# Cross network on one core: product 3 by seven small products in one more layer of pair A, layer 4 of pair B summed by DMA, the next input's transposes held back

## The chip, the cores and the metric

The kernel runs on one core of a Trainium2 chip. Five engines work side by side and wait for each other by semaphores: TensorE (PE in the profile, matmuls into PSUM), VectorE (DVE), ScalarE (ACT), GpSimd (POOL) and SyncE (SP). Here ScalarE copies every matmul result from PSUM to SBUF, VectorE does the sums and multiplications on SBUF, SyncE issues all ordinary DMAs and the transposing ones, and GpSimd issues the DMAs that add to what lies in SBUF. Each engine works through its own instructions in program order. The metric is the device time of one execution in microseconds.

## The reference

```
B, F, D, L = 16384, 100, 16, 6          # Din = 1024, all bf16
x = x0
for l in range(L):
    proj = x @ ws[l] + bs[l]            # 16384x1024 by 1024x1024
    x = x0 * proj + x
```

## The kernel before, in words

**Tiling.** The 16384 rows are cut into 16 pairs of 1024 rows; a pair has two halves n = 0, 1 of 512 rows. States are kept transposed (features on partitions), so a pair's input x0T and its state xst are each a tile `big` of 128 x 2 x 8 x 512. Eight rounds s = 0 to 7 each take two pairs, A and B, through the six layers, alternating: A0, B0, A1, B1 and so on to A5, B5. One such step (pair, layer) is the unit of this text. Six `big` tiles hold the inputs and states of A and B and the next inputs; the next round's inputs go to the tiles nA and nB.

**Products.** A step's 1024x1024 by 1024x1024 product is made in seven half-size products (1 to 7) instead of eight, from sums of weight blocks and sums T13, T2, T4 of the state. From round 1 on, some of the seven are themselves made from seven products of 256x256 blocks: product 2 (`in2`), product 4 (`in4`) and product 3 (`in3`, `X.l, in3 = l, s > 0 and l < L - 1`, so in layers 0 to 4). A product by four matmul groups is `mm` (line 450, 512 columns); by seven small ones it is `inner` (line 458, 256 columns). Each needs block sums of the state by VectorE (`ti2`, `ti4`, `ti3`), combinations of the weights (ids 8, 9 and 10 for products 2, 4 and 3), and sums of partial results (`EA` and `EB`; `E4` and `e5`; `E3` and `e6`).

**Weights.** In round 0 the combinations are made by VectorE (`combo`) and written to the DRAM tensor `Lc` by a DMA on SyncE; combination 10 of layer l is made in step B l. From round 1 on, nine 512 KB weight tiles per layer come through a ring of nine buffers (`prefetch_upto`), loaded in B steps as the buffers of the layer come free, and combination 10 comes by `load_third` into the tile P2s (line 365), which has a single buffer.

**The end of a step.** A step leaves its result in P1s, U2s, S53, P5s and C2; the state's new value is x0 times a projection, plus the old state. This is finished partly in the step itself (`fin_of`: m0, a0) and partly in the next step of the other pair (`trail`: m1, s11, a1, mC2, aC2). For the layers that `by_dma` names, `return 0 < Y.l < L - 1 - Y.pr % 2`, three of the four sums are not VectorE's but DMAs that add to xst, issued by GpSimd (`dadd`, line 50): one from T2 in the step itself, then one from U2s (m1d) and one from C2 (m2d, shown as `cb`) in the next step. Y.pr is odd for pair B, so A has it in layers 1 to 4, B in layers 1 to 3.

**Inputs and outputs.** `bring` loads the next pair's input by two transposing DMAs (`load_x0`, line 224). It is called from the list `pending`, which a step runs right after it has asked for its first weights, so before nearly all of its other work: in A5 `bring("A")`, and in rounds 1 to 6 `bring("B")` too. In round 0 the input of B is brought at the start of the next step A0. A finished pair is turned back by a transposing DMA from xst to x0T (`turn_pair`, line 351, called by `end_of(Y, True)` in the next step, after `w6 = weights(6)`), and written out by two DMAs (`write_pair`, line 358) at the start of the step after that. All of these stand in SyncE's one queue, in the order in which the program calls them.

Of the kernel before, what the change touches and what calls it, by code (L numbers as in the profile page):

```python
# [17 lines left out]
def kernel(  # L18
# [7 lines left out]
    nc = tc.nc  # L26
    P = nc.NUM_PARTITIONS
    B, D = x0.shape
    L = ws.shape[0]
# [6 lines left out]
    NPAIR = B // PR  # L36
# [6 lines left out]
    pin = tc.keep_in_program_order  # L43

    def vtt(out, in0, in1, op):
        return pin(nc.vector.tensor_tensor(out=out, in0=in0, in1=in1, op=op))  # L46
# [27 lines left out]
    def bigt(i):  # L74
        return big.tile([P, 2, KD, NB], BF16, name=f"big{i}")
# [4 lines left out]
    def bank(p):  # L80
        return p.tile([P, NB], FP32, name="px")
# [17 lines left out]
    def prefetch_upto(n):  # L99
        while state["next"] < min(n, len(keys)):  # L100
            k = keys[state["next"]]
            W[k] = wtile()
            pin(nc.sync.dma_start(W[k][:], raw_src(k[1], k[2]) if k[2] in RAW else lc(k[1], k[2])))
            state["next"] += 1
# [6 lines left out]
    def alloc(l):  # L111
        for pid in (1, 2, 4):
            W[0, l, pid] = wtile()
        for i, pid in enumerate((6, 3, 7)):
            W[0, l, pid] = wtile() if l % 2 == 0 else quarter(extra, i)
        W[0, l, 8] = quarter(extra, 3)

    def load_raw(l, eng, pids):
        for pid in pids:
            if pid == 12:  # L120
                t = raw12[l] = ei_pool.tile([P, KH, H], BF16, name="ea")
            else:
                t = W[0, l, pid]
            pin(eng.dma_start(t[:], raw_src(l, pid)))

    def combo(l, pid):
        if pid <= 7:
            a, op, b = {5: (lambda: raw12[l], ADD, lambda: W[0, l, 4]), 6: (lambda: W[0, l, 5], SUB, lambda: W[0, l, 1]),
                        3: (lambda: W[0, l, 2], SUB, lambda: W[0, l, 6]), 7: (lambda: W[0, l, 1], SUB, lambda: raw12[l])}[pid]
            if pid == 5:  # L130
                W[0, l, 5] = ei_pool.tile([P, KH, H], BF16, name=("eb", "e4")[l % 2])
            t = W[0, l, pid]
            vtt(t[:], a()[:], b()[:], op)
        else:
            w = W[0, l, {8: 2, 9: 4, 10: 3}[pid]]
            t = W[0, l, 8] if pid == 8 else ti_pool.tile([P, KH, H], BF16, name="ti4")
            i11, i12, i21, i22 = w[:, 0:2, 0:HE], w[:, 0:2, HE:H], w[:, 2:4, 0:HE], w[:, 2:4, HE:H]
            iv = t[:].rearrange("p k (j e) -> p k j e", e=HE)
            vtt(iv[:, 0], i12, i22, ADD)
            vtt(iv[:, 3], i11, i12, SUB)  # L140
            vtt(iv[:, 1], iv[:, 0], i11, SUB)
            vtt(iv[:, 2], i21, iv[:, 1], SUB)
        pin(nc.sync.dma_start(lc(l, pid), t[:]))
# [65 lines left out]
    home = dict(xA=0, xB=1, sA=2, sB=3, nA=4, nB=5)  # L209
# [11 lines left out]
    def load_x0(pr, x0T):  # L221
        for n in range(2):
            r0 = pr * PR + n * NB
            pin(nc.sync.dma_start_transpose(out=x0T[:, n], in_=x0[r0:r0 + NB, :]))
# [28 lines left out]
    new = {}  # L253
    prev = None
    pending = []
# [44 lines left out]
                None if Y.l == 0 else (lambda: vtt(eh1(Y.xst), C2[:], eh1(Y.src_in), ADD))]  # L300

    def by_dma(Y):
        return 0 < Y.l < L - 1 - Y.pr % 2

    def fin_of(Y, C, eh, n):
        xs = half(eh)
# [56 lines left out]
    def load_third(l):  # L363
        third[l] = evt("P2s")
        pin(nc.sync.dma_start(third[l][:], lc(l, 10)))

    for s in range(NPAIR // 2):
        for l in range(L):
            for side in ("A", "B"):
                X, Y = cur[side], prev  # L370
                first, last = step == 0, (X.pr, l) == LAST
                in2, in4 = not first, s > 0 and not (s + 1 == NPAIR // 2 and l + 1 == L)
                X.l, in3 = l, s > 0 and l < L - 1
                psA, psX = ps[step % 2], ps[1 - step % 2]
                step += 1
                bias = lambda eh, m, l=l: b_all[:, l * KD + eh * KH + m: l * KD + eh * KH + m + 1]
                if l == 0:
                    if side == "A" and s > 0:
                        home = dict(xA=home["nA"], xB=home["nB"], sA=home["sA"], sB=home["sB"], nA=home["xA"], nB=home["xB"])
                    X.xst = bigt(home["s" + side])  # L380

                def bring(who, s=s, home=home):
                    pr = 2 * (s + 1) + (who == "B")
                    new[who] = Pair(pr, bigt(home["n" + who]))
                    load_x0(pr, new[who].x0T)

                if side == "B" and s + 1 < NPAIR // 2 and l == L - 1:
                    pending.insert(0, lambda: load_third(0))
                if side == "A" and s + 1 < NPAIR // 2:
                    if l == L - 1:  # L390
                        pending.append(lambda: bring("A"))
                        if s > 0:
                            pending.append(lambda: bring("B"))

                if s + 1 == NPAIR // 2 and side == "A" and l == 2:
                    x0R = bigt(home["nA"])[:].rearrange("p n k b -> p (n k b)").rearrange("p (j d) -> p j d", d=D)
# [24 lines left out]
                def weights(pid):  # L421
                    if s == 0:
                        if l == L - 1 and side == "B":
                            prefetch_upto({1: 6, 2: 7}.get(pid, 8))
                        elif l == L - 1 and pid == 7:
                            prefetch_upto(6)
                        return W[0, l, pid]
                    k = (s, l, pid)
                    if side == "B":
                        prefetch_upto(pos[k] + RING)  # L430
                    else:
                        prefetch_upto(pos[s, l, ORDER[-1]] + 1)
                    return W[k]
# [29 lines left out]
                def evi(dst, pt):  # L463
                    acopy(dst, pt[:].rearrange("p (m b) -> p m b", m=2))
# [16 lines left out]
                pending = []  # L481
# [10 lines left out]
                for f in order:  # L492
                    if f is not None:
                        f()
                if in2:
                    q2, q5, q1 = bank(psX), bank(psX), bank(psX)
                    w2i = weights(8)
# [115 lines left out]
                late = nl == 0 and side == "A" and s == 1  # L613
# [12 lines left out]
                if s == 0:  # L626
                    if side == "A":
                        if l > 0 and l + 1 < L:
                            alloc(l + 1)
                        if l + 1 < L:  # L630
                            load_raw(l + 1, nc.sync, (12, 4, 1, 2) if l > 0 else (12,))
                        for pid in ((5, 6, 3) if 0 < l < L - 1 else ()):
                            combo(l + 1, pid)
                        combo(l, 9)
                    elif l + 1 < L:
                        for pid in (5, 6, 3) if l == 0 else ():
                            combo(1, pid)
                        combo(l + 1, 7)
                        combo(l + 1, 8)
                        combo(l, 10)  # L640
                w6 = weights(6)
                end_of(Y, True)
                if last:
# [5 lines left out]
                if in4:  # L649
# [41 lines left out]
                    if in3:  # L691
                        inner(cols(y1), wk[:, 3], t3[:, 2], False)
                        evi(e3[1, 0], y1)
                        if side == "B" and l + 1 < L - 1:
                            load_third(l + 1)
                    else:
                        inner(cols(z1), wj[:, 3], t4[:, 2], False)
                        evi(e4[1, 0], z1)
# [95 lines left out]
```

## Time and profile before

| | us |
|---|---|
| median of 3 runs (2240.04 to 2242.85) | 2240.09 |
| the profiled execution: its time | 2241.76 |
| its span | 2240.0 |
| TensorE busy in the span | 2217.2 (99%) |
| VectorE busy | 2145.2 (96%) |
| ScalarE busy | 2013.8 (90%) |
| GpSimd busy | 146.2 (7%) |

A row of the timeline has the start in us, the duration, the engine, the line, the operation, output <- input, and how many instructions are merged; what stands in brackets is the idle time before and what ended it. SPq is SyncE's queue: the duration there is the time that SyncE was held by issuing a DMA, not the time to landing. In the view by stretches each row has the stretch, its length, the busy time of each engine with its number of instructions, TensorE's granted clock, the DMA engines' busy share and their rate. Matmuls overlap, so their spacing is read from the starts and not from the durations.

### The profile page before, as it was taken

The numbers are of one execution on the slowest core, as the hardware profiler recorded it, in microseconds if no ns is written. First come the engines' busy times: TensorE is split into PE (matmuls) and PEld (weight loads), VectorE is DVE, ScalarE is ACT, GpSimd is POOL, SyncE is SP. The second block draws the span as 40 slices with busy tenths as digits, with TensorE's granted clock in tenths as the row PEclk, the third lists the DMA queues.
The fourth block names the chain that finished last, engine by engine and source line by source line (L and its number), as shares of the span: only waits on it lengthen the run. The fifth ranks groups of instructions, "written<-read, shape, count | busy, mean of one in ns | idle before, by whom it ended". The sixth has DMA issues, their size and how long they took to land.

```text
span 2240.0 us, 36436 instructions
## 1 busy us (share of the span) xinstructions
PE 2217.2 (99%) x13503; PEld 1346.1 (60%) x13765; DVE 2145.2 (96%) x2797; ACT 2013.8 (90%) x3587; POOL 146.2 (7%) x178
## 2 busy tenths in 40 slices
PE   9999999999999999999999999999999999999999
PEld 4555556665666656666566665666656666566664
DVE  7888989999999999999999999999999999999999
ACT  6777789998999989999899998999989999899996
POOL 0011000110000100011000110001100110001100
PEclk9999999999999999999999999999999999999999
DMA  7676697768966689666996668956789667987777
GB/s 234 193 194 178 193 211 209 187 160 207 238 205 169 160 223 249 193 156 166 228 249 182 160 177 224 267 151 160 195 219 254 155 165 207 209 243 198 177 200 179
DMA packets 538453, 443.85 MB, mean 198 GB/s; under 512 B 393890, under 2 KB 473764, under 8 KB 538276
## 3 DMA queue, kind: packets, MB, share of 16 engines
q1 hardware_dynamic: 514020, 353.41, 54.4%
q0 software_dynamic: 24192, 88.09, 21.7%
q8 instruction: 108, 1.77, 0.3%
q14 instruction: 69, 0.57, 0.1%
q10 hardware_dynamic: 64, 0.01, 0.0%
HBM read 232.27 MB, written 55.05 MB: 128 GB/s over the span
## 4 chain that ended last, share of the span: by engine, by line
PE 96%; DVE 2%; DMA 1%; issue 1%; SPq 0%; ACT 0%; DVEq 0%; ACTq 0%
PE px L450 62%; PE px L458 33%; DVE cb L46 1%; DMA P2s<-Lc 0%; DVE big L46 0%; DVE S L46 0%; DVE T L46 0%; DMA b_rows<-in_bs_dram 0%; DVE P1s L46 0%; PE px L232 0%; DVE P5s L46 0%; DVE ti L46 0%; DVE ea L46 0%; DVE e L46 0%; PE px L238 0%
## 5 line engine op out<-in xcount | busy, mean ns | idle before, releaser
L450 PE MATMUL px<-T,wp 128*128 128x512 bf16 x4219 | 1059.4, 379 | 7.7
L450 PEld LDWEIGHTS <-wp 128*128 128x128 bf16 x6224 | 608.9, 98 | 507.3 <-issue 0.6
L458 PEld LDWEIGHTS <-wp 128*128 128x128 bf16 x5592 | 547.2, 98 | 263.8
L59 ACT ACTIVATE cb<-px,b_all 128x512 bf16<-128x512 f32 x760 | 502.6, 687 | 55.8 <-PE px L450 38.2
L458 PE MATMUL px<-ti,wp 128*128 128x256 bf16 x2964 | 444.7, 273 | 0.1
L450 PE MATMUL px<-big,wp 128*128 128x512 bf16 x1759 | 440.4, 379 | 4.4
L56 ACT CAST e<-px 128x512 bf16<-128x512 f32 x608 | 352.5, 618 | 19.1 <-PE px L458 19.1
L56 ACT CAST ea<-px 128x512 bf16<-128x512 f32 x344 | 201.4, 585 | 76.5 <-PE px L458 75.2
L56 ACT CAST U2s<-px 128x512 bf16<-128x512 f32 x384 | 231.9, 604 | 19.5 <-PE px L450 17.9
L59 ACT ACTIVATE P1s<-px,b_all 128x512 bf16<-128x512 f32 x376 | 243.3, 696 | 4.2 <-PE px L450 2.7
L458 PE MATMUL px<-big,wp 128*128 128x256 bf16 x1644 | 246.6, 273 | 0.0
L59 ACT ACTIVATE S<-px,b_all 128x512 bf16<-128x512 f32 x380 | 243.6, 693 | 1.0 <-PE px L450 0.5
L46 DVE TENSOR_TENSOR T<-big,T 128x2048 bf16<-128x2048 bf16 x192 | 234.5, 1222 | 1.2
L56 ACT CAST P5s<-px 128x512 bf16<-128x512 f32 x384 | 225.1, 595 | 11.1 <-PE px L450 5.7
L46 DVE TENSOR_TENSOR T<-big 128x4096 bf16<-128x4096 bf16 (+2 forms) x98 | 219.7, 2242 | 2.4 <-PE px L450 1.6
L46 DVE TENSOR_TENSOR cb<-cb,big 128x2048 bf16<-128x2048 bf16 (+3 forms) x145 | 194.1, 1340 | 0.4
L56 ACT CAST eb<-px 128x512 bf16<-128x512 f32 x258 | 153.6, 595 | 0.7
L50 POOL DMA_DIRECT2D big<-T x56 | 48.3, 863 | 1508.6 <-DVE T L46 1508.6
L46 DVE TENSOR_TENSOR S<-U2s,S 128x2048 bf16<-128x2048 bf16 (+1 forms) x97 | 117.6, 1213 | 26.1 <-ACT U2s L56 26.1
L46 DVE TENSOR_TENSOR ti<-big,ti 128x512 bf16<-128x512 bf16 x332 | 139.7, 421 | 0.4
L458 PEld LDWEIGHTS <-P2s 128*128 128x128 bf16 x1120 | 109.5, 98 | 43.4 <-DMA P2s<-Lc 0.8
L458 PE MATMUL px<-T,wp 128*128 128x256 bf16 x984 | 134.2, 273 | 0.1
(88 smaller groups left out, 1984.3 us busy)
## 6 DMA issues: line engine op xcount, KB each, us to landing
wp<-Lc SPq DMA_DIRECT2D x252, 512.0 KB, 6.1
wp<-in_ws_dram SPq DMA_DIRECT2D x144, 512.0 KB, 5.9
big<-T POOLq DMA_DIRECT2D x56, 512.0 KB, 5.0
big<-U2s POOLq DMA_DIRECT2D x56, 512.0 KB, 5.6
big<-cb POOLq DMA_DIRECT2D x56, 512.0 KB, 7.7
out_dram<-big SPq DMA_DIRECT2D x28, 1024.0 KB, 10.9
P2s<-Lc SPq DMA_DIRECT2D x35, 512.0 KB, 6.7
Lc<-big SPq DMA_DIRECT2D x15, 512.0 KB, 4.1
```

The costliest lines, as they stand in the source:

```text
L46: return pin(nc.vector.tensor_tensor(out=out, in0=in0, in1=in1, op=op))
L50: pin(nc.gpsimd.dma_start(out=out, in_=in_, accum_op=ADD))
L56: return pin(nc.scalar.copy(out=out, in_=in_))
L59: return pin(nc.scalar.activation(out=out, in_=in_, func=IDENT, bias=bias, scale=1.0))
L450: nc.tensor.matmul(pts[m][:], lhsT=wt[:, k, m * P:(m + 1) * P], rhs=rhs[:, k, :], start=(start and k == 0), stop=(k == KH - 1), **kw)
L458: nc.tensor.matmul(dst(m), lhsT=w[:, k, m * P:(m + 1) * P], rhs=rhs[:, k, :], start=(start and m == 0 and k == 0), stop=(k == 1), skip_gro ...
```

## The change

Product 3 is made by seven products also in A5 of rounds 1 to 6. For that, combination 10 of layer 5 is made in B5 of round 0 and written to `Lc`, and `load_third(5)` is issued in every B4 from round 1 on. `by_dma` now holds for layer 4 of pair B too, in all rounds, so its sums run as DMAs in B4 and A5. In rounds 1 to 6 the next inputs are no longer brought at the start of A5, but after the step's VectorE sums have been called; a 1x2 memset on GpSimd, written to the new input tile, stands in GpSimd's queue behind the U2s and cb sums, and the transposes wait for it. Round 0 still brings A at the start of A5.

```diff
     def by_dma(Y):
-        return 0 < Y.l < L - 1 - Y.pr % 2
+        return 0 < Y.l < L - 1
...
-                X.l, in3 = l, s > 0 and l < L - 1
+                X.l, in3 = l, s > 0 and (l < L - 1 or (side == "A" and s + 1 < NPAIR // 2))
...
-                def bring(who, s=s, home=home):
+                def bring(who, s=s, home=home, late=False):
                     pr = 2 * (s + 1) + (who == "B")
                     new[who] = Pair(pr, bigt(home["n" + who]))
+                    if late:
+                        pin(nc.gpsimd.memset(new[who].x0T[0:1, 0, 0, 0:2], 0.0))
                     load_x0(pr, new[who].x0T)
...
                 if side == "A" and s + 1 < NPAIR // 2:
-                    if l == L - 1:
+                    if l == L - 1 and s == 0:
                         pending.append(lambda: bring("A"))
-                        if s > 0:
-                            pending.append(lambda: bring("B"))
...
                 for f in order:
                     if f is not None:
                         f()
+                if l == L - 1 and side == "A" and 0 < s < NPAIR // 2 - 1:
+                    bring("A", late=True)
+                    bring("B")
...
                         combo(l + 1, 7)
                         combo(l + 1, 8)
                         combo(l, 10)
+                    else:
+                        combo(l, 10)
                 w6 = weights(6)
...
-                        if side == "B" and l + 1 < L - 1:
+                        if side == "B":
                             load_third(l + 1)
```

## The prediction

> **What bounds the kernel now.** I read the page first (busy shares, chain), then the stretches step by step, then SyncE's queue where the change moves DMAs. A step is one layer of one pair, A0 to A5 and B0 to B5 in each of eight rounds (0 to 7), cut where ScalarE starts its first copy into P1s; + is us after that cut. The page:
>
> ```profile
> span 2240.0 us, 36436 instructions
> PE 2217.2 (99%) x13503; PEld 1346.1 (60%) x13765; DVE 2145.2 (96%) x2797; ACT 2013.8 (90%) x3587; POOL 146.2 (7%) x178
> PE 96%; DVE 2%; DMA 1%; issue 1%; SPq 0%; ACT 0%; DVEq 0%; ACTq 0%
> ```
>
> TensorE sets the time; VectorE has 4% to spare. The stretches, one step each: A4, A5 and B5 of round 3, and B5 of round 0:
>
> ```profile
> core 0: us, PE busy (x) PEld busy (x) DVE busy (x) ACT busy (x) POOL busy (x), PEclk, DMA share, GB/s
> 1035.04:1058.02 22.98, 22.82 (x147) 14.47 (x148) 22.49 (x32) 21.57 (x41) 2.58 (x3) 1.00 0.53 138
> 1080.99:1104.37 23.38, 23.22 (x135) 13.30 (x137) 23.28 (x27) 20.13 (x37) 0.00 (x0) 1.00 1.15 220
> 1104.37:1127.75 23.38, 23.28 (x136) 13.32 (x137) 23.15 (x26) 20.09 (x37) 0.00 (x0) 1.00 0.85 208
> 272.55:296.33 23.78, 23.67 (x124) 12.15 (x125) 19.56 (x19) 18.66 (x32) 0.00 (x0) 1.00 1.00 247
> ```
>
> A step with product 3 by seven products takes 22.98, without it 23.38. VectorE has 0.5 us spare in the first kind, 0.1 in A5, but 4.2 in B5 of round 0. SyncE's queue from there on (start, duration):
>
> ```profile
> 281.15 10.55 SPq L351 DMA_TRANSPOSE big<-big  x1
> 295.41 0.32 SPq L103 DMA_DIRECT2D wp<-Lc  x1
> 295.78 9.45 SPq L224 DMA_TRANSPOSE big<-in_x_dram  x2
> 305.33 5.03 SPq L358 DMA_DIRECT2D out_dram<-big  x2
> 310.46 14.70 SPq L351 DMA_TRANSPOSE big<-big  x1
> 325.26 0.53 SPq L103 DMA_DIRECT2D wp<-in_ws_dram  x1
> 327.06 5.43 SPq L358 DMA_DIRECT2D out_dram<-big  x2
> 332.58 5.17 SPq L103 DMA_DIRECT2D wp<-in_ws_dram  x1
> 337.85 1.92 SPq L103 DMA_DIRECT2D wp<-Lc  x4
> 341.50 0.80 SPq L365 DMA_DIRECT2D P2s<-Lc  x1
> ```
>
> Here SyncE is idle from 291.7 to 295.4 and then issues back to back for 46 us, but for 1.3 us before 327.06. What that does to TensorE in A1 of round 1 (starts at 343.2):
>
> ```profile
> 347.68 1.03 PE L450 MATMUL px<-T,wp 128*128 128x512 bf16 x4
> 350.28 0.60 PE L458 MATMUL px<-big,wp 128*128 128x256 bf16 x4
> 351.43 0.61 PE L458 MATMUL px<-big,P2s 128*128 128x256 bf16 x4 [0.55 <-DMA P2s<-Lc]
> ```
>
> It is TensorE's only wait in mid-run. The P2s load was issued at 341.50, landed at 351.39, and was used at +8.25; all other steps use it at +7.43.
>
> **The change, part by part.**
>
> *Product 3 in A5, rounds 1 to 6.* 16 matmuls of 512 columns become 28 of 256. By starts, four of 512 take 0.87 us and four of 256 take 0.43: 3.47 against 3.03, 0.43 less. By steps it is 23.38 - 22.98 = 0.40. I take 0.40, as it holds all that comes with it: **-2.4 us** in six steps (bound by matmuls -2.6). That is 0.11% of the time: even undisturbed, it is inside the 0.2% that I take as the least that a measurement tells from no change.
>
> *VectorE in A5 and B4.* A5 gains the ti3 and e3 sums (3 us) and the S53 sum (1.14 by starts), and loses the sums now made by DMA. What results is B4's load of today: 22.49 plus the one sum a0 (1.14) = 23.63, over 22.98. B4 runs so without a wait, because VectorE works ahead: its T13 starts at -2.59 before B4's end eats that down to -1.45 at A5's start. After the change B4 loses a0, A5 starts at -2.59 and B5 at -1.45 (today -2.39). Cost 0; the cover is T13's 2.3 us, done at +0.8, against product 5, which needs it at +2.7.
>
> *What B5's lateness delays.* The turn of pair A waits for VectorE's last sum in B5 and is issued at +12.82; it moves by 0.94. A0's T13 moves from -3.11 to -2.36 (it now waits 0.13 for TensorE there), so the turn of pair B moves by 0.75. Behind them on SyncE stand the output writes, then A1's weights and P2s, the last landing 1.55, about 2.0, 0.06, 1.20, 1.94 and 2.88 us ahead of use in rounds 2 to 7. Shifted by about 0.85, only round 4 goes short: **+0.8** (0 to 3, if the tight round is another each time).
>
> *24 more accumulating DMAs and the hold.* GpSimd pays 0.86 us each and is 7% busy. In A5 they go out at +1.36 (U2s) and +4.30 (cb), so the 1x2 memset and with it the four transposes start at +5.3 instead of -0.6. Their issue took 6.28, 6.36, 4.20 and 4.73 us, so SyncE is free at B5 +3.8. Behind it wait B5's first weight load (today +2.52) and load_third(0) (+2.97): both are used a step or more later (P2s with 23 us to spare), and the next load, at +5.99, is on time. Cost 0. The new x0 lands at about B5 +7; VectorE first reads it at +15. The cb DMA (7.8 us to landing) must be read out before ScalarE writes cb again at +16.5, so 4.4 us are spare; that no DMA of this kind ever ran beside a transpose in the trace leaves it open (rival 2). In round 0 the transposes are not held; the sums there have until +19.4. load_third(5) goes out at B4 +21 and is used at A5 +7.43, as in other layers with 2 to 3 us spare. In round 7 it is loaded for nothing, and the turn behind the DMA sums there (+12.2 for its data, today issued at +13.0) is no later.
>
> *combo(5,10) in B5 of round 0.* Four sums of 0.42 us, 1.4 by starts:
>
> ```profile
> 288.67 0.42 DVE L46 TENSOR_TENSOR ti<-big,ti 128x512 bf16<-128x512 bf16 x1
> 289.13 1.23 DVE L46 TENSOR_TENSOR S<-U2s,S 128x2048 bf16<-128x2048 bf16 x1
> 291.96 2.29 DVE L46 TENSOR_TENSOR T<-big 128x4096 bf16<-128x4096 bf16 x1 [1.61 <-PE px L450]
> ```
>
> On VectorE they fit the 1.61 us of idle time. But their write to Lc stands on SyncE *ahead* of the turn of pair A (L351). SyncE waits for the last sum, at about 290.5 (289.0 + 1.4), and issues a 0.32 us write; the turn starts at 291.0, not 281.15, and ends at 301.6. The load behind it waited for its buffer till 295.41: it goes out 6.2 us later. From there to 341.5 nothing on the queue waits for an engine that has slack, so the 6.2 us reach A1's loads; they land 1.27 us apart, as fast as the DMAs deliver. P2s lands at 357.6, TensorE needs it at 350.6: 7.0 us of waiting against 0.82, **+6.2** (0 if the queue catches up, 8 if the delayed transposes are as slow as the 6.3 us ones in A5). About 4.6 of it falls on the pid 2 weights (342.2 + 6.2, needed at 343.8).
>
> Sum: -2.4 + 0.8 + 6.2 = +4.6. The profiled execution took 2241.76 us for a span of 2240.0; the median of the three runs is 2240.09, 1.7 less. The difference applied to the median: **2244.7**.
>
> **The rivals.**
> 1. *The queue catches up (other side).* The 14.70 and 5.17 us issues are long because the queue is full; the median turn takes 11.4, a load 0.4. If a later start shortens them, 3.3 + 4.8 = 8 us come back, P2s is in time, and 2240.1 - 2.4 = 2237.7. It decides once 3.8 us are won back. Against: the queue is full of the same writes, in the same order.
> 2. *Transposes hold up the sums.* If cb's DMA waits for one and a half transposes (4.6 each), it lands at 12.1 + 6.9 = +19.0, 2.5 after ScalarE wants cb, six times: 2244.7 + 15 = 2259.7. It starts to cost at 4.4 us of delay. For it: A5's DMA share is 1.15 already. The Trainium skill ("DMA: Bandwidth & Descriptors", Queues, rings and completion order) speaks against it: each DMA engine alternates between queues packet by packet; no row here shows it.
> 3. *TensorE slows after its wait.* The eight matmuls at the start took 0.45 us each:
> ```profile
> 1.20 3.60 PE L232 MATMUL px<-zero 128*128 128x512 bf16 x8 [1.20 <-DVE zero L204]
> ```
> against 0.22 in mid-run. If 4.6 us of idling brings that rate back, the 6.8 us of work before P2s cost up to 6.8 more, of which 2.4 are hidden behind P2s. I take 2 more: 2246.7. By the Trainium skill ("TensorE: Matmul & The Clock Gate", Part 1: The HAM clock gate) an idle window of about 3.4 us halves the clock, and 3.4 us of work restore it: an estimated 1.7 us, all hidden.
> 4. *VectorE becomes the bound in A5*: 23.63 instead of 23.38, +0.25 where -0.40 was counted: 3.9 more in six steps, 2248.6. Against: B4 carries that load today.
>
> **How the numbers follow.** Forecast 0.60 (its own range 2243 to 2246.5), rivals 0.12, 0.12, 0.08 and 0.06, 0.02 for what I don't see. Leaving out rival 2 and the rest, the range is 2237.5 to 2250. Slower by over 0.2% begins at 2244.57: some 0.53 of the forecast lies above, with rivals 2, 3 and 4 that makes 0.57. Within 0.2%: rival 1 and the rest of the forecast, 0.41. Faster: 0.02, as nothing here is worth 4.5 us.
>
> **What would show it.** A5 of rounds 1 to 6 at 22.98; T13 of B5 at -1.45; the four transposes after A5 +5.3; in round 0 the turn at 291 and P2s at about 347; A1 of round 1 near 30 us with TensorE waiting on weights and P2s. I am wrong if A1 of round 1 stays near 23.7, or if A5 shows ScalarE waiting to write cb.

## The result, and the profile after

| | before | after |
|---|---|---|
| median, us | 2240.23 (2239.21 to 2242.85) | 2245.93 (2245.14 to 2247.69) |
| ratio to before, 95% interval | | 1.0025 (1.0016 to 1.0035) |
| the profiled execution: its time | 2241.76 | 2247.28 |
| its span | 2240.0 | 2245.3 |
| A5 of rounds 1 to 6, each | 23.38 | 22.98 |
| B5 of rounds 1 to 6, each | 23.38 | 23.38 |
| A1 of round 1 | 23.71 | 33.06 |
| A0 of round 0 (the first step) | 27.34 | 25.82 |
| B5 of round 7 (the last step) | 29.54 | 29.07 |

The changed kernel is slower by 5.7 us. Every other step is as long as before, so the table holds the whole difference of the spans: 9.35 lost in A1 of round 1, 2.40 won in six A5, and 2.0 that lie in the first and the last step (1.5 of them is the load of `b_rows`, on which the first step waited 0.4 us here and 1.9 before; that wait differs from one execution to the next). 9.35 - 2.40 - 1.5 - 0.5 = 5.0, and 5.3 with the 0.3 by which the starts of the first steps differ.

The page of the changed kernel: the span, TensorE's and the other engines' busy time, and the chain of work that ended last.

```profile
span 2245.3 us, 37014 instructions
PE 2233.3 (99%) x13837; PEld 1354.5 (60%) x13837; DVE 2140.9 (95%) x2835; ACT 2022.6 (90%) x3611; POOL 167.0 (7%) x208
PE 99%; DMA 1%; DVE 0%; ACT 0%; SPq 0%; issue 0%
```

TensorE is still the bound, and its share tells nothing of the 5.7 us. What does is the view by stretches. The rows are A5 and B5 of round 3, B5 of round 0 and A1 of round 1:

```profile
core 0: us, PE busy (x) PEld busy (x) DVE busy (x) ACT busy (x) POOL busy (x), PEclk, DMA share, GB/s
1088.35:1111.32 22.97, 22.97 (x150) 14.46 (x149) 22.39 (x32) 21.56 (x40) 1.75 (x3) 1.00 1.10 253
1111.32:1134.70 23.38, 23.38 (x138) 13.30 (x137) 23.28 (x27) 20.13 (x36) 0.00 (x0) 1.00 1.08 250
271.37:295.16 23.79, 23.79 (x126) 12.13 (x125) 20.91 (x23) 18.66 (x32) 0.00 (x0) 1.00 0.62 204
342.01:375.07 33.06, 27.40 (x150) 15.41 (x149) 21.22 (x30) 21.66 (x41) 0.86 (x1) 0.85 0.54 177
```

A5 has the length of the other steps with product 3 by seven. In A1 of round 1 TensorE is idle for 5.66 us (33.06 - 27.40), and it is the one step in mid-run with a granted clock below 1: 0.85. Its 150 matmul records kept it busy for 27.40 us instead of 22.98.

SyncE's queue from B5 of round 0 on (columns: start, time that SyncE was held, line, operation, how many):

```profile
289.41 0.32 SPq L143 DMA_DIRECT2D Lc<-ti  x1
289.82 10.45 SPq L351 DMA_TRANSPOSE big<-big  x1
300.37 0.53 SPq L103 DMA_DIRECT2D wp<-Lc  x1
...
315.97 14.13 SPq L351 DMA_TRANSPOSE big<-big  x1
...
338.52 4.91 SPq L103 DMA_DIRECT2D wp<-in_ws_dram  x1
343.53 2.26 SPq L103 DMA_DIRECT2D wp<-Lc  x4
346.86 0.49 SPq L365 DMA_DIRECT2D P2s<-Lc  x1
```

The write to `Lc` (L143) stands first, and SyncE does nothing until VectorE has made the last of the four sums. Counted from the step's start (the steps start 1.2 earlier in this execution), the turn of pair A is issued at +18.44 instead of +8.60, 9.84 later; the idle time that SyncE had there takes up 3.7, so that the load behind the turn goes out 6.1 later, P2s 6.5. TensorE in A1 of round 1, with the idle time before a row and what ended it in brackets:

```profile
347.40 1.03 PE L458 MATMUL px<-big,wp 128*128 128x256 bf16 x4 [4.64 <-DMA wp<-in_ws_dram]
349.38 1.03 PE L458 MATMUL px<-ti,wp 128*128 128x256 bf16 x4 [0.95 <-DMA wp<-Lc]
350.20 1.91 PE L450 MATMUL px<-big,wp 128*128 128x512 bf16 x4
...
355.32 0.60 PE L458 MATMUL px<-big,wp 128*128 128x256 bf16 x4
...
358.36 0.60 PE L458 MATMUL px<-big,wp 128*128 128x256 bf16 x4
358.80 2.07 PE L450 MATMUL px<-T,wp 128*128 128x512 bf16 x8
360.70 0.60 PE L458 MATMUL px<-big,P2s 128*128 128x256 bf16 x4
```

Three things are to be seen. TensorE waits for the weights twice, 5.6 us together. After the first wait four matmuls of 256 columns take 1.03 us until 355.3, and 0.60 from then on. Stretches of the same kernel around these rows (the number after POOL is the granted clock):

```profile
349.40:351.40 2.00, 2.00 (x7) 1.01 (x8) 2.00 (x3) 0.95 (x2) 0.00 (x0) 0.50 1.03 422
355.40:357.40 2.00, 2.00 (x15) 1.28 (x14) 0.69 (x1) 1.71 (x4) 0.00 (x0) 1.00 0.89 354
```

The clock was halved, for 10.24 us. So TensorE came to P2s at +18.69, some 3.4 us after it had landed (about +15.3: its landing is not recorded, its neighbours' are +14.09 and +16.59), without waiting for it.

The third thing is the order. In all other steps, and in this one before the change, the four matmuls with P2s follow right behind the four of `big,wp`; here eight of 512 columns come first. The matmuls are in another order in this program, in this step alone; e8 below, the same program once more, has them in this order again. It covers 1.72 us (8 x 0.215) of a late P2s, and costs some of it again: from the first use of P2s to the end of the step there are 14.4 us here against 15.5 before, so 1.1 are won.

### The profile page after: what moved, and what is told of

Same layout as the page of the kernel before. It is cut to its first block, busy times and chain, and to the rows that moved or that the text cites. A ratio compares the mean times of both kernels' runs of the same rounds, so it can differ in the third digit from the quotient of the medians.

```text
span 2245.3 us, 37014 instructions
## 1 busy us (share of the span) xinstructions
PE 2233.3 (99%) x13837; PEld 1354.5 (60%) x13837; DVE 2140.9 (95%) x2835; ACT 2022.6 (90%) x3611; POOL 167.0 (7%) x208
## 4 chain that ended last, share of the span: by engine, by line
PE 99%; DMA 1%; DVE 0%; ACT 0%; SPq 0%; issue 0%
PE px L450 63%; PE px L458 34%; PE px L445 1%; DMA wp<-Lc 0%; DMA b_rows<-in_bs_dram 0%; DVE cb L46 0%; PE px L232 0%; SPq L103 0%; PE px L238 0%; PE px L442 0%; PE px L440 0%; ACT S L59 0%; ACT cb L56 0%; ACT e L56 0%; ACT U2s L56 0%
## 5 line engine op out<-in xcount | busy, mean ns | idle before, releaser
L450 PE MATMUL px<-T,wp 128*128 128x512 bf16 x4384 | 1083.0, 379 | 0.0
L458 PE MATMUL px<-ti,wp 128*128 128x256 bf16 x2988 | 449.3, 273 | 1.0 <-DMA wp<-Lc 0.9
L450 PE MATMUL px<-big,wp 128*128 128x512 bf16 x1744 | 426.4, 380 | 0.0
L56 ACT CAST e<-px 128x512 bf16<-128x512 f32 x632 | 366.3, 620 | 20.5 <-PE px L458 20.5
L458 PE MATMUL px<-big,wp 128*128 128x256 bf16 x1692 | 254.7, 273 | 4.6 <-DMA wp<-in_ws_dram 4.6
L46 DVE TENSOR_TENSOR cb<-cb,big 128x2048 bf16<-128x2048 bf16 (+2 forms) x153 | 194.8, 1275 | 1.0 <-ACT cb L56 0.5
L50 POOL DMA_DIRECT2D big<-T x64 | 55.2, 863 | 1443.6 <-DVE T L46 1420.7
L458 PEld LDWEIGHTS <-P2s 128*128 128x128 bf16 x1216 | 119.0, 98 | 46.6 <-issue 0.3
L46 DVE TENSOR_TENSOR ti<-big,ti 128x512 bf16<-128x512 bf16 x345 | 144.5, 419 | 0.5
L458 PE MATMUL px<-ti,P2s 128*128 128x256 bf16 x912 | 136.8, 273 | 0.0
```

What stands on the lines that cost most here:

```text
L50: pin(nc.gpsimd.dma_start(out=out, in_=in_, accum_op=ADD))
L56: return pin(nc.scalar.copy(out=out, in_=in_))
L450: nc.tensor.matmul(pts[m][:], lhsT=wt[:, k, m * P:(m + 1) * P], rhs=rhs[:, k, :], start=(start and k == 0), stop=(k == KH - 1), **kw)
L458: nc.tensor.matmul(dst(m), lhsT=w[:, k, m * P:(m + 1) * P], rhs=rhs[:, k, :], start=(start and m == 0 and k == 0), stop=(k == 1), skip_gro ...
```

## The experiments

Times in the text with a + are counted from the step's start, as in the prediction; the turn's are counted from the start of B5 of round 0.

**e1: the turn first.** The same sums, called behind the end of the step instead of ahead of it:

```diff
-                    else:
-                        combo(l, 10)
                 w6 = weights(6)
                 end_of(Y, True)
+                if s == 0 and l == L - 1 and side == "B":
+                    combo(l, 10)
```

> The changed kernel with combo(5,10) called after the turn of pair A, so that the write to Lc stands behind the turn on SyncE. My theory (the order on SyncE's queue, and TensorE's halved clock after the wait, make the whole loss): the turn of round 0 starts near 280 us again, A1 of round 1 takes 23.7 us as before the change (33.06 in the changed kernel), TensorE's clock stays full, the six A5 stay at 22.98, and the time is 2240.2 - 2.4 = 2237.8 us (2236.5 to 2239). Rival (24 more summing DMAs and the held transposes load the DMA engines, and the loss sits there): A1 stays near 33 us, the time within 1 us of 2245.9.

Measured: 2238.29 us, ratio to before 0.9989 (0.998 to 0.9997). The turn starts at +8.60 as before, A1 of round 1 takes 24.93, every A5 22.98. TensorE's waits of this kernel have one line of that step:

```profile
PE px L458 <- DMA P2s<-Lc: 1.7, 1, 1.7
```

One line of code moved takes 8 us away, in the times as in A1's length (33.06 - 24.93 = 8.1). What is left of the change gains. A1 was expected at 23.7: 24.93 is long for this place of the turn, as in other runs below that leave the turn there, e7 apart, it took 23.1 (e5) to 23.9 (e11).

**e2: the write alone.** The kernel before, with nothing of the change but combination 10 of layer 5:

```diff
                         combo(l, 10)
+                    else:
+                        combo(l, 10)
                 w6 = weights(6)
```

> The kernel before, with nothing of the change but combo(5,10) and its write in B5 of round 0 (its result is not used). My theory: A1 of round 1 takes 33 us (32 to 34), with TensorE idle some 4.6 us and then at half clock; all other steps as before; 2240.2 + 9.3 = 2249.5 us. Rival (the sums by DMA and the held transposes are needed for the loss): A1 stays at 23.7 and the time at 2240.2.

Measured: 2249.78 us, ratio 1.004 (1.0027 to 1.0054). A1 of round 1 takes 31.45; TensorE's wait and the stretch of that step:

```profile
PE px L458 <- DMA wp<-in_ws_dram: 5.2, 1, 5.2
```

```profile
342.51:373.96 31.45, 25.98 (x150) 14.91 (x149) 21.21 (x30) 21.61 (x40) 0.86 (x1) 0.89 0.58 188
```

A1 was expected at 32 to 34, so 31.45 is a little less. A5 and B5 stay at 23.38. The write alone makes the loss, with the halved clock (0.89 in the mean) in it. One other step of this execution is longer than before: A1 of round 4 takes 23.61 instead of 22.98, as P2s came late there too.

**e3: TensorE kept busy.** The changed kernel, with 22 matmuls of zeros in A1 of round 1 where TensorE would wait:

```diff
                     mm(1, w1, pA, 2, True)
+                    if (s, l, side) == (1, 1, "A"):
+                        for _ in range(22):
+                            nc.tensor.matmul(q5[:], lhsT=zero[:, 0:P], rhs=zero[:], start=True, stop=True)
                     inner(cols(q1), wr[0, 0], b[0, 0], True)
```

> The changed kernel with 22 matmuls on the zero tile (22 x 0.217 = 4.8 us at full clock) in A1 of round 1, ahead of the matmul that waits for the late weights, into a bank that is written anew afterwards. My theory (3.3 us of the loss are the halved clock): the clock stays at 1.0, P2s lands at the same time near 357.4 and is then what TensorE waits for; A1 takes 22.98 + (357.4 - 350.6) = 29.8 us, the time is 2245.9 - 3.3 = 2242.6. Rival (the weights come one by one, and the slow matmuls only fill the time between them): A1 stays at 33 us, the time at 2245.9.

Measured: 2246.45 us, ratio 1.0027 (1.0016 to 1.0038); A1 of round 1 takes 32.03, where 29.8 was expected. TensorE there, and the step's stretch:

```profile
342.75 4.91 PE L519 MATMUL px<-zero 128*128 128x512 bf16 x22
347.64 0.61 PE L458 MATMUL px<-big,wp 128*128 128x256 bf16 x4
...
358.73 0.61 PE L458 MATMUL px<-big,P2s 128*128 128x256 bf16 x4 [2.61 <-DMA P2s<-Lc]
```

```profile
342.16:374.19 32.03, 28.23 (x172) 16.38 (x171) 21.46 (x30) 21.79 (x40) 0.86 (x1) 1.00 0.57 184
```

The filler did what it was put there for: the clock stays at 1.00 and four matmuls take 0.61 right after it. The expected 29.8 was wrongly worked out: its 357.4 is from the changed kernel's execution, where A1 starts at 342.0, and its 350.6 from the kernel before, where it starts at 343.2. Counted from the step's start the same sum is 22.98 + 15.3 - 7.43 = 30.9. P2s follows right behind `big,wp` again in this kernel's order, as that sum takes it, but lands at about +16.5, 1.2 later than in the changed kernel: 30.9 + 1.2 = 32.1, and 32.03 was measured. Why P2s came later in this execution is open. The time is that of the changed kernel, as the rival had it. So e3 shows that the clock can be held up, and does not tell what that is worth in the times, since the order and P2s' landing changed too.

**e4: half as late.** The four sums called earlier in the step, right behind the sum of P1s and EA:

```diff
                     vtt(P1s[:], P1s[:], EA[:], ADD)
+                    if s == 0 and l == L - 1 and side == "B":
+                        combo(l, 10)
...
-                    else:
-                        combo(l, 10)
                 w6 = weights(6)
```

> The changed kernel with combo(5,10) called earlier in B5, right after the sum of P1s and EA; the write still stands ahead of the turn, but its sums end about 3.7 us earlier (at +14.3), so the turn ends at about +25.3 and the load behind it is 2.5 us late instead of 6.2. My theory: A1 of round 1 is longer than before by those 2.5 us alone, 23.7 + 2.5 = 26.2, no single wait of TensorE reaches 3 us, the clock stays full, and the time is 2245.9 - (33.1 - 26.2) = 2239.0. Rival (a write ahead of the turn costs the same whenever it comes, or any wait brings the half clock): A1 at 30 us or more, 2243 or above.

Measured: 2242.35 us, ratio 1.0008 (0.9999 to 1.0017), against 2239.0 expected; A1 of round 1 takes 28.00 instead of 26.2. The turn starts at +14.83. TensorE in A1:

```profile
345.54 0.61 PE L458 MATMUL px<-big,wp 128*128 128x256 bf16 x4 [2.23 <-DMA wp<-in_ws_dram]
```

The lateness moves with the turn's start, as it should. The miss is in its size: the load behind the turn goes out 3.0 later than before (expected 2.5), P2s 4.4 later, and P2s lands at about +12.5, 4.3 later than before. 23.71 + 4.3 = 28.0 is the step's length. The clock was at half for 3.41 us in this step, though TensorE's longest wait was 2.23 and the expectation had it full; it cost next to nothing, as P2s was used as soon as it had landed.

**e8: the changed kernel again**, for the spread of A1 of round 1:

> The changed kernel once more, as it is, to see how far the late step moves from one execution to another. My theory: A1 of round 1 is again 32 to 34 us with one wait of 4 us or more for the pid 2 weights and half clock behind it, 2246 us. Rival (the 33.06 us were one bad execution): below 31 us.

Measured: 2246.52 us, ratio 1.0026 (1.0016 to 1.0035). A1 of round 1 takes 30.93, not the 32 to 34 expected but just what the rival had (below 31): TensorE waits 4.99 for the weights, but the clock is at half for 3.41 us instead of 10.24. The times of the two series are alike even so (2246.52 and 2245.93). The profiled execution of the changed kernel is one of its longer ones (2247.28), and the one of e8 the shortest of its series (2245.58).

The runs on the turn together, sorted by its start. Where the profile lists no landing of P2s ("about") it is taken between its neighbours, and in e1, e3 and e4 as the last of the sixteen counts of its semaphore in the trace. "Used" is the start of the first matmul with it. e7 comes below:

| kernel | turn starts | P2s lands | P2s used | half clock, us | A1 of round 1 |
|---|---|---|---|---|---|
| e7 | +8.60 | +5.48 | +7.54 | 0 | 22.98 |
| before | +8.60 | +8.21 | +8.25 | 0 | 23.71 |
| e1 | +8.60 | about +9.4 | +9.48 | 0 | 24.93 |
| e4 | +14.83 | about +12.5 | +12.54 | 3.41 | 28.00 |
| e8 (as changed) | +18.44 | about +15.4 | +16.57 | 3.41 | 30.93 |
| e2 | +18.44 | +16.00 | +17.09 | 6.83 | 31.45 |
| e3 | +18.44 | about +16.5 | +16.57 | 0 | 32.03 |
| changed | +18.44 | about +15.3 | +18.69 | 10.24 | 33.06 |

The changed kernel, e8 and e2 have the order with eight matmuls ahead of P2s, and so need it at +9.15; the others at +7.43, when its weight load begins (the first matmul follows at +7.54). A turn later by 9.84 brings P2s later by 7.1 to 8.3 (by 5.9 to 7.1, if e1 is what one compares with). The use follows the landing, and where the clock was halved it comes up to 3.4 us behind it.

**e7: the output of pair B one step later.** With e1's order, the two output DMAs of pair B, which stand ahead of A1's loads on SyncE, are called in A1 instead of B0:

```diff
-    pending = []
+    pending, held = [], []
...
-                pending = []
+                pending, held = held, []
...
-                    pending.append(lambda Y=Y: write_pair(Y))
+                    (held if Y.pr % 2 else pending).append(lambda Y=Y: write_pair(Y))
```

> e1_turn_first, and pair B's output is written one step later, in A1, where SyncE loads nothing, instead of between the turn of pair B and B0's weight loads. My theory (what is left of the wait in A1 of round 1 comes from the full queue before the weights): P2s in A1 lands 3 us or more ahead of its use in rounds 2 to 7, A1 of round 1 has no wait and takes 22.98 (24.93 in e1_turn_first's profile, 23.71 before the change), time 2238.3 - 1.3 = 2237.0 us. Rival (the loads are late because of the turn, not of the writes): A1 of round 1 stays above 23.7, time 2238.3.

Measured: 2237.53 us, ratio 0.9984 (0.9975 to 0.9992): faster than both kernels. All waits of TensorE in this execution:

```profile
PE px L232 <- DVE zero L204: 1.2, 1, 1.2
PE px L247 <- DMA b_rows<-in_bs_dram: 0.4, 1, 0.4
PE px L450 <- DVE T L46: 0.2, 1, 0.2
```

Two lie in the first step and none in A1. P2s lands 1.65 to 3.1 us ahead of its use in rounds 2 to 7, in some rounds less than the 3 us expected.

**e6: without the DMA sums of layer 4 of pair B.** e1 with `by_dma` as before the change:

```diff
-        return 0 < Y.l < L - 1
+        return 0 < Y.l < L - 1 - Y.pr % 2
```

> e1_turn_first with layer 4 of pair B summed by VectorE as before the change (by_dma as before). My theory (VectorE has no room for product 3's sums in A5 otherwise): VectorE's work in A5 is 2.1 us and in B4 1.1 us more, T13 of B5 and of the next B0 start at about +1.2 and +1 instead of -1.45 and -0.8, TensorE waits for them, about 1.1 us in each of six rounds: 2238.3 + 6.6 = 2245 us (2241 to 2249). Rival (VectorE works far enough ahead): 2238.3 +- 1.5.

Measured: 2247.38 us, ratio 1.0029 (1.0018 to 1.0041), 9 us more than e1. TensorE waits for VectorE:

```profile
PE px L450 <- DVE T L46: 7.4, 12, 0.8
```

A5 takes 22.98 even so, but VectorE hands its arrears on: T13 of B5 starts at +1.28 (with the DMA sums at -1.45), B5 takes 24.25 and B0 23.64. The DMA sums are what pays for product 3 by seven.

**e5: without the hold.** e1, with the four transposes of the next inputs called at the start of A5 in all rounds, as before the change:

```diff
-                    if late:
-                        pin(nc.gpsimd.memset(new[who].x0T[0:1, 0, 0, 0:2], 0.0))
...
-                    if l == L - 1 and s == 0:
+                    if l == L - 1:
                         pending.append(lambda: bring("A"))
+                        if s > 0:
+                            pending.append(lambda: bring("B"))
...
-                if l == L - 1 and side == "A" and 0 < s < NPAIR // 2 - 1:
-                    bring("A", late=True)
-                    bring("B")
```

> e1_turn_first with the hold taken away: in all rounds the next inputs are brought at the start of A5 again, ahead of the U2s and cb sums. My theory (the transposes do not hold up the sums; in round 0 of the changed kernel, where they are not held, the sums landed after 5.9 and 7.5 us and it was the transpose that took 13.3): A5 22.98 and B5 23.38 in rounds 1 to 6 as in e1_turn_first, time 2238.3 +- 1.5 us. Rival (the sums land behind the transposes, after +20 in A5): T13 of B5 or ScalarE's copies into cb wait, A5 + B5 is 1 us or more longer in each of six rounds, 2244 or above.

Measured: 2378.38 us, ratio 1.0624 (1.0596 to 1.0652). A5 takes 43 to 51 us in rounds 1 to 6. Two waits of this kernel (in total, times, longest), and SyncE's queue in A5 of round 2:

```profile
ACT U2s L56 <- DMA big<-U2s: 132.4, 6, 26.4
PE px L458 <- ACT e L56: 127.5, 6, 25.6
```

```profile
826.17 46.14 SPq L224 DMA_TRANSPOSE big<-in_x_dram  x4
```

ScalarE may not write U2s until the sum has read it, and TensorE waits for ScalarE. The two sums land 28 to 36 us after their issue; the first transpose holds SyncE for 29 to 38 us. My theory for this run is refuted by far. In the meantime the DMA engines are not idle but slow (stretch of A5 in round 2; last columns: granted clock, DMA share, GB/s):

```profile
846.00:852.00 6.00, 0.00 (x0) 0.00 (x0) 0.00 (x0) 0.00 (x0) 0.00 (x0) 0.50 1.27 57
```

**e9: held behind one sum.** e1, with the transposes called behind the U2s sum but ahead of the cb sum:

```diff
-                if l == L - 1 and side == "A" and 0 < s < NPAIR // 2 - 1:
-                    bring("A", late=True)
-                    bring("B")
...
                 for f in order:
                     if f is not None:
                         f()
+                    if f is m1 and l == L - 1 and side == "A" and 0 < s < NPAIR // 2 - 1:
+                        bring("A", late=True)
+                        bring("B")
```

> e1_turn_first with the transposes held behind the U2s sum alone: they start at A5 +2.3, and the cb sum is issued at +4.3 in the middle of the first transpose, as both sums are in round 0. Theory 1 (a sum that is issued while a transpose is under way is held up by it, as in e5_no_hold): cb lands after 20 us or more, A5 takes 35 us or more in rounds 1 to 6, 2320 us or above. Theory 2 (it takes more than that, as in round 0, where the sums landed after 5.9 and 7.5 us in the middle of a transpose): cb lands after 7 to 10 us, A5 22.98, 2238.3 +- 1.5 us.

Measured: 2323.74 us, ratio 1.0369 (1.0338 to 1.0399); A5 takes 34 to 39 us. The U2s sum, issued 0.9 us ahead of the first transpose, lands 6.5 to 8.6 us after its issue; the cb sum, issued 2.0 us behind it (1.4 in round 6), after 23 to 28.

```profile
ACT cb L59 <- DMA big<-cb: 84.1, 6, 16.2
PE px L458 <- ACT cb L59: 72.1, 12, 13.7
```

So it is the sum issued behind the transposes that gets stuck. But in round 0, which the change leaves without a hold, both sums are issued behind the first transpose, and in the changed kernel they land 5.9 and 7.5 us after their issue. The last three runs ask why.

**e10: two transposes instead of four.** e5, with only pair A's called in A5, in all rounds, as in round 0; pair B's are called in the next A0:

```diff
                     if l == L - 1:
                         pending.append(lambda: bring("A"))
-                        if s > 0:
-                            pending.append(lambda: bring("B"))
...
-                    if s == 0:
+                    if side == "B" and s + 1 < NPAIR // 2:
                         pending.append(lambda bring=bring: bring("B"))
```

> The kernel of e5_no_hold, but only pair A's two transposes are called at the start of A5, in all rounds; pair B's two are called at the start of the next A0. So rounds 1 to 6 are now as round 0 always was, where two transposes beside the sums cost nothing (sums landing 5.9 and 7.5 us after their issue), but with weight loads instead of writes to Lc ahead of them on SyncE. Theory (it takes four transposes in a row: the collapse is a matter of how many stand in front): A5 of rounds 1 to 6 stays under 25 us, the sums land within 10 us, and the whole takes some 2238 to 2250 us. Rival (any transpose under way at the sums' issue does it, and round 0 escapes by what stands ahead on the queue): A5 takes 33 to 45 us in rounds 1 to 6, the sums land after 15 us or more, and the whole takes 2300 to 2370 us. A lengthening of A5 by half of what e5_no_hold showed (some 10 us) would mean that the cost goes by the number of transposes, without a threshold.

Measured: 2436.43 us, ratio 1.0873 (1.0843 to 1.0903). The sums land after 27 to 39 us, and A5 takes 42 to 54. It is not the number; the theory fell. (The rest of the loss is in A1 of rounds 2 to 7, 31 to 33 us, where the weights now stand behind pair B's transposes.) SyncE ahead of A5 of round 1:

```profile
524.13 0.43 SPq L365 DMA_DIRECT2D P2s<-Lc  x1
524.88 0.32 SPq L103 DMA_DIRECT2D wp<-Lc  x1
525.24 46.20 SPq L224 DMA_TRANSPOSE big<-in_x_dram  x2
```

Two differences from round 0 remain: there the first transpose starts 4.6 us ahead of the U2s sum (here 1.9), and no load was issued shortly ahead of it.

**e11: round 0 with the transposes later.** e1; in round 0 the transposes wait for ScalarE's first copy of A5:

```diff
-                    if late:
+                    if late is True:
                         pin(nc.gpsimd.memset(new[who].x0T[0:1, 0, 0, 0:2], 0.0))
+                    elif late:
+                        pin(nc.gpsimd.tensor_tensor(out=new[who].x0T[0:1, 0, 0, 0:2], in0=P1s[0:1, 0, 0:2], in1=P1s[0:1, 0, 0:2], op=ADD))
...
-                if side == "A" and s + 1 < NPAIR // 2:
-                    if l == L - 1 and s == 0:
-                        pending.append(lambda: bring("A"))
...
                 ev(P1s, pA, 0, None if first else 0)
+                if l == L - 1 and side == "A" and s == 0:
+                    bring("A", late="P1s")
```

> The kernel of e1_turn_first, but in round 0 the two transposes of pair A wait for ScalarE's first copy into P1s of A5 (by a two-element sum on GpSimd), so that they start some 1.9 us ahead of the issue of the U2s sum, as in the rounds that collapsed, instead of 4.6 us; no weight load is in flight there, only writes to Lc long before. Rounds 1 to 6 are held as before. Theory (the distance decides: a sum issued about 2 us after the first transpose gets stuck, one issued when it is nearly handed over does not): A5 of round 0 takes 35 to 55 us instead of 23.78, the U2s sum lands 20 us or more after its issue, the whole takes 2250 to 2270 us. Rival (the weight loads ahead of the transposes decide): A5 of round 0 stays under 25 us, the U2s sum lands within 9 us, the whole takes about 2238 us.

Measured: 2238.57 us beside 2239.88 of the kernel before, one run of each. The first transpose starts 1.35 us ahead of the U2s sum; the sums land after 6.8 and 7.3 us, A5 of round 0 takes 23.86.

```profile
249.71 12.87 SPq L224 DMA_TRANSPOSE big<-in_x_dram  x2
```

The distance does not decide; this theory fell too. No load is in flight here when the transposes start, but a write to `Lc` of 512 KB is: issued 3.38 us ahead of the first transpose, it lands 0.4 us after that has started.

**e12: round 0 with loads ahead.** e11 and two loads of 512 KB into tiles that are free in round 0:

```diff
                 if l == L - 1 and side == "A" and s == 0:
+                    for t in (ti_pool.tile([P, KH, H], BF16, name="ti3"), ei_pool.tile([P, KH, H], BF16, name="e3")):
+                        pin(nc.sync.dma_start(t[:], raw_src(5, 1)))
                     bring("A", late="P1s")
```

> The kernel of e11_round0_later with two loads of 512 KB (weight blocks, their result unused) on SyncE just ahead of pair A's transposes in A5 of round 0. Without them, in e11_round0_later, transposes that started 1.35 us ahead of the U2s sum cost nothing (sums landing 6.8 and 7.3 us after issue). Theory (loads still in flight when the transposes start are what brings the sums to a stop, as in rounds 1 to 6 of e5_no_hold, e9_hold_one and e10_two_only): a sum lands 15 us or more after its issue, A5 of round 0 takes 30 to 50 us instead of 23.9, the whole some 2245 to 2265 us. Rival (it is something else in which round 0 differs): the sums land within 10 us, A5 stays under 25 us, the whole takes about 2239 us.

Measured: 2249.86 us beside 2239.77 of the kernel before, one run of each. SyncE's queue and ScalarE's wait:

```profile
246.13 1.14 SPq L487 DMA_DIRECT2D ti<-in_ws_dram  x1
247.32 1.31 SPq L487 DMA_DIRECT2D e<-in_ws_dram  x1
249.14 27.82 SPq L224 DMA_TRANSPOSE big<-in_x_dram  x2
```

```profile
ACT U2s L56 <- DMA big<-U2s: 12.1, 1, 12.1
```

The second load lands at 253.61, 4.5 us after the first transpose has started. The sums now land after 22.4 and 22.3 us, A5 of round 0 takes 36.60 instead of 23.86, and the two transposes hold SyncE for 27.82 us instead of 12.87. This theory held: two loads in flight make the difference.

## Why the prediction was right, and where not

The time came out at 2245.9 where 2244.7 was forecast: slower by 5.7 against 4.6. That it came so near is in part luck, as the parts below show: 0.8 was counted that is not there, and 2.3 of a slow clock was left out; P2s came 0.9 later than forecast, and an order of the matmuls that nobody had planned gave 1.1 back.

**Product 3 in A5, -2.4: right.** Six times 22.98 instead of 23.38.

**VectorE's cover, 0: right.** T13 of B5 starts at -1.45, as the working had it, and A5 and B5 show no wait of TensorE for VectorE; rival 4 did not come. e6 shows how thin the cover is: without the DMA sums the same change costs 9 us.

**B5's lateness, +0.8: measured 0.** The turns did move (T13 of A0 is at -2.38, forecast -2.36). P2s lands 0.95, 1.80, 1.74, 0.49 and 0.84 ahead of its use in rounds 2, 3, 4, 6 and 7, and TensorE waits in none (in round 5 the landing is not recorded). The margins shrank, but the tight round 4 of before was not tight in this execution; the forecast had put one execution's margins into the sum. Single rounds do go short in other executions: A1 of round 7 takes 23.14 in e4, and A1 of round 4 takes 23.61 in e2, which has none of B5's lateness.

**The held transposes, 0: right.** They start at +5.22 (forecast +5.3). SyncE in A5 of round 1 of the changed kernel:

```profile
541.17 22.81 SPq L224 DMA_TRANSPOSE big<-in_x_dram  x4
```

It is free again 2.8 to 5.0 us into B5 (forecast +3.8), and the loads behind it are in time. The sums land 6.7 to 7.7 us after their issue, well ahead of what ScalarE needs.

**combo(5,10) ahead of the turn, +6.2: right in its mechanism and nearly in its size.** The turn started at +18.44 of B5 (forecast 291.0, which is +18.45 by the steps of before), the load behind it went out 6.1 later (forecast 6.2), and TensorE waited 4.64 for pid 2's weights (forecast 4.6); e1 and e2 show that the place of this one write is the cause, by taking it away and by adding it alone. Two things came in between that the working had not. P2s landed 7.1 later, not 6.2; and TensorE's changed order, which the prediction did not look at, gave 1.1 back. 7.1 - 1.1 = 6.0: without the next point A1 would have taken 23.71 + 6.0 = 29.7 ("near 30", as the prediction had it).

**Rival 3, TensorE slows after its wait: it happened, and is the term that was mis-sized.** The forecast's main case had it at 0, the rival at 2 with a chance of 0.08. With a full clock TensorE would have come to P2s 3.4 us earlier in the changed kernel, when it landed: 29.7 + 3.4 = 33.1, which is the step's length. In e3, with a full clock, TensorE stood ready for P2s 2.61 us before it could go on. By the same distance from landing to use the slow clock cost 1.2 in e8 (29.7 + 1.2 = 30.9, its length), 1.1 in e2 and next to nothing in e4. The two executions of the changed program give 2.3 in the mean, and -2.4 + 6.0 + 2.3 = +5.9 where the times say +5.7. In this working only the lengths are measured; the landings of P2s in the changed kernel and in e8 are taken between their neighbours, and no run changed the clock alone. The half-clock stretches last 3.41, 6.83 or 10.24 us, one, two or three times the same length.

Why one program lost 3.4 us in one execution and 1.2 in another can be read from the trace. The clock changes on a grid of 3.41 us, counted from the start of the first full-clock stretch (in the changed kernel it falls after 337.92 us, 99 such lengths; in e2, e4 and e8 after 341.33, 100 lengths). Cut along this grid, A1 of round 1 of the changed kernel looks like this (length, PE busy with its matmuls, granted clock, DMA share, GB/s):

```profile
341.66:345.07 3.41, 1.10 (x6) 1.00 0.93 204
345.07:348.49 3.42, 1.03 (x4) 0.50 0.93 328
348.49:351.90 3.41, 2.52 (x8) 0.50 1.02 413
351.90:355.31 3.41, 3.41 (x13) 0.50 1.07 400
```

The wait of 4.64 is spread over two lengths (2.31 and 2.38 us idle), the wait of 0.95 falls into the third, and only the fourth is fully busy; then the clock is back. In e8 a wait of 4.99 leaves 3.38 us idle in one length and 0.39 of other idling in the next, after which the clock is back already. Counted so in the fourteen traces of this case, by the matmul records, the clock fell after every length with 2.30 us or more of idling and after none with 1.98 or less; it came back after every length with 0.71 or less and after none with 0.84 or more. So e4's waits of 2.23 and 0.65, together in one length, halved the clock, while e3's wait of 2.61, split into 1.13 and 1.48 by the grid, did not. What a wait costs thus hangs on where it falls on the grid, and that differed between the two executions of one program.

The rule of the Trainium skill that was weighed there ("TensorE: Matmul & The Clock Gate", Part 1: The HAM clock gate) has a free-running window of about 3.4 us; after an idle one the clock is halved, after a busy one it is full again. The traces agree, but in them a window with 2.30 of its 3.41 us idle is idle enough. The prediction's estimate from it, 1.7 us and all hidden behind P2s, fell short: 3.4 and 1.2 us were lost after P2s had landed.

**Rival 1, the queue catches up: fell.** The 6.1 us of the load behind the turn became 6.5 at the issue of P2s and 7.1 at its landing; nothing was won back. The rival's time (2237.7) is what the kernel takes without the lateness: e1 2238.3, e7 2237.5.

**Rival 2, transposes hold up the sums: not here, but far from wrong.** It did not come because the transposes are held. Its mechanism exists: e5, e9, e10 and e12 show sums landing after 22 to 39 us, where the rival had put 14.7. The rule that was cited against it, of alternating packets ("DMA: Bandwidth & Descriptors", Queues, rings and completion order, in the Trainium skill), did not keep the sums of e5 from landing after 28 to 36 us, with the engines at 57 GB/s in the stretch shown. The packets in the trace do not speak against alternation as such, since neither side is shut out: from 846 to 848 us in e5, 22 packets of the sums and 282 of SyncE's queue start. Both are slow: in A5 of round 2 of the changed kernel 96 of the sums start from 820 to 822, and 1909 of SyncE's queue from 826 to 828, when the transposes have the engines alone. That the hold itself does useful work, which the prediction gave no price, is shown by e5: without it e1 would take 140 us more.

In all the runs that overlapped the three, the sums got stuck when two things held: a load was still in flight when the transposes started, and the sum was issued behind that start. With no load in flight (round 0, e11) or with the sum issued ahead (U2s in e9; both sums of the changed kernel, whose last load of B4 lands at 543.14 in round 1, after the transposes' start at 541.17) they landed in 6 to 9 us. A write to `Lc` in flight did not do it (e11). The pattern is shown, for the loads by one run of e12; how the queues bring it about is open, since no row shows why a packet waits. Loads and transposes without sums do not do it: before the change they stood so in A5 of rounds 1 to 6, and each transpose was handed over in 3.8 to 7.5 us.

## What to carry to other kernels

A DMA whose data is late holds up everything behind it on its queue, so a new write belongs behind the transfers that the next steps wait for: one line moved was worth 8 us here, three times what the whole change gains. When work is added to an engine that is full, find what pays for it (here the sums by DMA, 9 us) and what protects that in turn (here the hold, 140 us), and price each by taking it away alone. A margin read from one execution is no term of a sum; take it as a range.

## What the runs showed of the hardware that was not expected

- Accumulating DMAs (GpSimd, 512 KB, SBUF to SBUF) issued while transposing DMAs (SyncE, DRAM to SBUF) are under way and loads ahead of these are still in flight land after 22 to 39 us instead of 4.5 to 10, and a transpose then holds SyncE for up to 40 us instead of 4 to 10. Without the loads (e11), or with the sums issued 0.9 us ahead of the transposes (the changed kernel), this did not happen. Why is open.
- TensorE's granted clock changed on a grid of 3.41 us: in the fourteen traces it fell to half after each length of the grid with 2.30 us or more of idling (none with 1.98 or less) and rose after each with 0.71 or less (none with 0.84 or more). A wait of 2.23 us was enough when a second one of 0.65 fell into the same length (e4), and one of 2.61 was not when the grid split it (e3).
